# Loading the first K tile ahead of WQ and W1 in a DMA-bound attention decode kernel

## The chip, the cores and the metric

One core of a Trainium2 chip. The metric is the device time of one execution in microseconds (us). Within a comparison both kernels ran on the same chip; the experiments came in two batches on two chips, and the kernel before took 1272.90 us in one and 1272.82 us in the other. The changed kernel itself was not run again in these batches; where an experiment is set against it, the kernel before (1272.86 us beside it) is the link.

## The reference

The output mixes two branches with a gate: attention of one new token over a long K/V cache, and a small dense block.

```python
q = (x @ wq)                                     # x: 2 x 1 x 448, 16 query heads of 256
scores = einsum(q, repeat(k_cache, 2)) / 16      # k_cache: 2 x 8 x 32768 x 256, bf16
a = (softmax(scores) @ repeat(v_cache, 2)) @ wo  # v_cache: the same size
b = gelu(x @ w1 + b1) @ w2 + b2                  # 448 -> 1792 -> 448
g = sigmoid(sum(x * gate_w))
return g * a + (1 - g) * b
```

K and V are 268 MB each. Each byte of them is used once, so the kernel is a stream of loads with a little work behind it.

## The kernel before

In what follows PE is the matrix engine, DVE the vector engine, ACT the scalar engine, and SP the engine whose queue issues the big loads. Q is x @ WQ, and H is x @ W1, from which the GELU chain starts.

K and V are cut into 32 tiles each (128 partitions x 64 KB, 8.4 MB). A ring of three slots in on-chip memory takes them in turn. WQ and W1 first lie together in slot 0.

```python
        order = [("WQ", 0), ("W1", 0)]
        for i in range(NTILES + LAG):            # NTILES 32, LAG 2
            if i < NTILES:
                order.append(("K", i))
            if i >= LAG and i - LAG < LASTV:
                order.append(("V", i - LAG))
        # ... (tail: last V, W2, WO)
        rot = [d for d in order if d[0] in "KV" and d != ("V", LASTV)]
        for n, d in enumerate(rot):
            slot_of[d] = (n + 1) % NB            # NB 3: K0 slot 1, K1 slot 2, K2 slot 0, V0 slot 1, K3 slot 2, V1 slot 0
        # ...
        def released(d):                         # what frees the slot of tile d
            kind, idx = d
            return {"K": ("S", idx, NCK // 2 - 1), "V": ("PV", idx), "WQ": "QT", "W1": "HT"}[kind]
```

The load queue (SP) issues loads in that order and waits, before each, until the slot's last user is done:

```python
            for d in order:
                for pd in before_of[d]:          # the tiles that lay in the slot before
                    E.wait("pe", released(pd))
                # ... issue the load of d
```

So K2 waits for Q and H, which read WQ and W1 in slot 0; V0 for the scores of K0; K3 for the scores of K1; V1 for the scores of K2.

DVE has to transpose each K tile in place (eight instructions) before PE can compute its scores. Its program is in fixed order:

```python
            # prog_dve ... mask, gate (gp, gs, g, dg) ...
            E.wait_total("d_b")                            # the biases
            E.ins(... b2_f <- b2_bf)
            E.wait("pe", "GG")                             # gate matmuls; PE does them after Q
            E.ins(... g32); E.ins(... omB)
            gelu1()                                        # begins with E.wait("pe", "HT"): all of H
            gelu2()
            for i in range(LAG):
                K(i)                                       # wait for the K tile, 8 transposes; softmax at each group's end
            E.loop((NTILES - LAG) // UNIT, steps, ("dve", ("PT", 0)))
```

PE's program is in fixed order too: Q (waits for WQ), gate matmuls, H (waits for W1), then the scores of K0, and so on.

Of the kernel before, what the change touches and what calls it, by code (L numbers as in the profile page):

```python
# [125 lines left out]
def bass_gated_mix__gqa_block_cached__dense_activation_gelu__decode_kernel(  # L126
# [40 lines left out]
    NTILES = NG * NT  # L167
# [33 lines left out]
    with contextlib.ExitStack() as es:  # L201
# [70 lines left out]
        W_WQ, W_W1 = KC * HD + HW, KC * Fd + HF  # L272
        assert W_WQ + W_W1 <= SLOT and (NC + FC) * Dm <= SLOT
        LASTV = NTILES - 1
        order = [("WQ", 0), ("W1", 0)]
        for i in range(NTILES + LAG):
            if i < NTILES:
                order.append(("K", i))
            if i >= LAG and i - LAG < LASTV:
                order.append(("V", i - LAG))  # L280
# [561 lines left out]
```

## Time and profile before

The kernel took 1272.86 us in the median of six runs (1272.69 to 1272.92).

These lines are from the page of the kernel before: the span, the busy time of the engines, and, for 40 equal slices of the span, the busy tenths of the 16 DMA engines and the rate in GB/s.

```profile
span 1270.7 us, 8089 instructions
...
PE 701.6 (55%) x4544; PEld 146.4 (12%) x2016; DVE 685.8 (54%) x528; ACT 43.7 (3%) x183; POOL 3.3 (0%) x14
...
DMA  9999999999999999999999999999999999999998
GB/s 405 444 430 435 428 432 433 434 431 438 431 431 429 441 433 433 435 431 433 429 435 437 433 433 435 431 431 429 441 433 433 431 435 431 431 435 437 433 422 371
```

PE and DVE are about half idle; DMA is full in 39 of the 40 slices (the last is the kernel's end). The trace's DMA packets say it more sharply: a tile is 128 packets of 64 KB, each 2.42 us on one of the 16 engines, so 433 to 434 GB/s and 19.35 us a tile. Between 20 and 1200 us there is never a moment with fewer than 16 packets under way.

The chain of waits looks as if it named another limit (second line: share of the span by line):

```profile
DMA 63%; DVE 19%; PE 15%; issue 3%; SPq 0%; another core or an unknown queue 0%
DMA ring<-in_A_k_cache_dram 59%; DVE ring L722 17%; PE ps_s L490 5%; PE ps_s L335 4%; PE ps_o L335 4%; DMA ring<-in_A_wo_dram 3%; DVE mx L726 1%; PE ps_o L539 1%; PE ps_m L504 0%; PE ps_m L499 0%; DVE gmax L728 0%; DVE gmx L732 0%; SPq L383 0%; SPq L376 0%
```

It puts 17% on the transposes. To see whether they cost time, look at how early the loads are queued. The last number of these lines, from the DMA view, is the median time from issue to landing in us:

```profile
ring<-in_A_k_cache_dram SPq DMA_DIRECT2D x32, 49.7
ring<-in_A_v_cache_dram SPq DMA_DIRECT2D x31, 36.6
```

A tile needs 19.35 us of transfer. In the median a V load is therefore issued some 17 us, and a K load some 30 us, before the engines reach it. A transpose that ends later eats this slack first.

The part of the run that the change touches, on DVE (start in us, duration in us, instruction, in brackets the idle time before it and what ended that):

```profile
27.00 0.38 DVE L715 SCALAR_TENSOR_TENSOR hT_bf<-u_sb,omB,z_sb 128x14 bf16<-128x14 f32 x2
36.36 17.66 DVE L722 STREAM_TRANSPOSE ring<-ring 128x2048 uint32<-128x2048 uint32 x8 [8.99 <-DMA ring<-in_A_k_cache_dram]
55.72 17.66 DVE L722 STREAM_TRANSPOSE ring<-ring 128x2048 uint32<-128x2048 uint32 x8 [1.69 <-DMA ring<-in_A_k_cache_dram]
...
82.78 17.66 DVE L722 STREAM_TRANSPOSE ring<-ring 128x2048 uint32<-128x2048 uint32 x8 [0.23 <-DVE PT L739]
```

and on the load queue, in order WQ, W1, then K0 to K2, V0, K3, V1:

```profile
0.74 0.88 SPq L371 DMA_DIRECT2D ring<-in_A_wq_dram  x2
1.67 1.11 SPq L376 DMA_DIRECT2D ring<-in_B_w_dram  x2
2.81 22.79 SPq L393 DMA_DIRECT2D ring<-in_A_k_cache_dram  x3
57.76 0.33 SPq L393 DMA_DIRECT2D ring<-in_A_v_cache_dram  x1
77.11 0.33 SPq L393 DMA_DIRECT2D ring<-in_A_k_cache_dram  x1
104.17 0.33 SPq L393 DMA_DIRECT2D ring<-in_A_v_cache_dram  x1
```

The GELU chain is over at 27.4 us, DVE then idles 9 us for K0, and the transposes of K1 start as soon as K1 has landed (55.7). V1 is issued at 104.17 us. The engines finish their last packets of K3 between 111.4 and 113.7 us, so V1 is 7 us early.

### The profile page before, as it was taken

The page shows a single profiled execution, that of the slowest core. Times are in us where ns is not written, and L with a number is a line of the kernel's source. Part 1 is how long each engine was busy: PE and PEld are TensorE (multiplying, and loading weights), DVE is VectorE, ACT ScalarE, POOL GpSimd, SP SyncE. Part 2 cuts the span into 40 slices and gives each one's busy share as a digit, 9 for nine tenths or more (in the row PEclk, how much of TensorE's full clock was granted, in tenths as well). Part 3 has the DMA queues.
Part 4 walks back from the last instruction along what each step waited for, and adds up shares of the span by engine and source line. Part 5 has one row for each costly group of instructions (what it writes and reads, how often), then busy time and mean ns, then how long its engine had stood idle before and what let it go on. Part 6 is the DMA issues. An engine that isn't in the chain of part 4 may idle for free.

```text
span 1270.7 us, 8089 instructions
## 1 busy us (share of the span) xinstructions
PE 701.6 (55%) x4544; PEld 146.4 (12%) x2016; DVE 685.8 (54%) x528; ACT 43.7 (3%) x183; POOL 3.3 (0%) x14
## 2 busy tenths in 40 slices
PE   4666556644476454665545665445664436655465
PEld 3111111100011100111100111000110001111012
DVE  2875536655365563556735466453665636556341
ACT  1000000000000000000000000000000000000000
POOL 1000000000000000000000000000000000000000
PEclk9987788767787767887777787678877778876787
DMA  9999999999999999999999999999999999999998
GB/s 405 444 430 435 428 432 433 434 431 438 431 431 429 441 433 433 435 431 433 429 435 437 433 433 435 431 431 429 441 433 433 431 435 431 431 435 437 433 422 371
DMA packets 11116, 547.61 MB, mean 431 GB/s; under 512 B 1368, under 2 KB 1632, under 8 KB 2144
## 3 DMA queue, kind: packets, MB, share of 16 engines
q1 hardware_dynamic: 10948, 547.43, 99.7%
q8 instruction: 9, 0.15, 0.0%
q10 hardware_dynamic: 156, 0.01, 0.0%
q14 instruction: 3, 0.02, 0.0%
HBM read 547.43 MB, written 0.00 MB: 431 GB/s over the span
## 4 chain that ended last, share of the span: by engine, by line
DMA 63%; DVE 19%; PE 15%; issue 3%; SPq 0%; another core or an unknown queue 0%
DMA ring<-in_A_k_cache_dram 59%; DVE ring L722 17%; PE ps_s L490 5%; PE ps_s L335 4%; PE ps_o L335 4%; DMA ring<-in_A_wo_dram 3%; DVE mx L726 1%; PE ps_o L539 1%; PE ps_m L504 0%; PE ps_m L499 0%; DVE gmax L728 0%; DVE gmx L732 0%; SPq L383 0%; SPq L376 0%
## 5 line engine op out<-in xcount | busy, mean ns | idle before, releaser
L722 DVE STREAM_TRANSPOSE ring<-ring 128x2048 uint32<-128x2048 uint32 x256 | 565.2, 2275 | 385.1 <-DMA ring<-in_A_k_cache_dram 384.8
L490 PE MATMUL ps_s<-ring,Abd 128*128 128x512 bf16 x1024 | 426.5, 416 | 424.1 <-DVE ring L722 423.7
L335 PE MATMUL ps_s<-ring,Abd 128*128 128x512 bf16 x1024 | 422.5, 413 | 0.0
L490 PEld LDWEIGHTS ps_s<-ring,Abd 128*128 128x128 bf16 x1024 | 106.1, 104 | 846.8 <-DVE ring L722 475.4
L335 PE MATMUL ps_o<-ring,PT 128*24 128x512 bf16 x1504 | 115.4, 415 | 0.0
L539 PE MATMUL ps_o<-ring,PT 128*24 128x512 bf16 x544 | 58.9, 432 | 14.0 <-DMA ring<-in_A_v_cache_dram 14.0
L509 PE MATMUL ps_f<-o_sb,selg 128*32 128x257 f32 x32 | 17.0, 634 | 83.5 <-DVE o_sb L763 83.5
L763 DVE SCALAR_TENSOR_TENSOR o_sb<-ps_o,mask,o_sb 128x256 f32<-128x256 f32 x112 | 54.1, 483 | 9.9 <-PE ps_o L539 6.0
L726 DVE TENSOR_REDUCE mx<-ps_s 128x1 f32<-128x1024 f32 x16 | 19.6, 1224 | 59.8 <-PE ps_s L335 59.8
L636 ACT ACTIVATE negm<-ps_m 128x1 f32<-128x1 f32 x16 | 2.7, 171 | 1155.9 <-PE ps_m L504 1155.9
L739 DVE STREAM_TRANSPOSE PT<-pexp 128x1024 bf16<-128x1024 bf16 x16 | 19.9, 1244 | 41.1 <-PE ps_o L335 41.1
L539 PEld LDWEIGHTS ps_o<-ring,PT 128*24 128x24 bf16 x544 | 14.8, 100 | 108.0 <-issue 89.3
L736 DVE COPY ls<-lsum 128x1 f32<-128x1 f32 x16 | 2.5, 154 | 32.3 <-ACT pexp L640 32.3
L630 ACT COPY Abd<-qrep 32x16 bf16 (+1 forms) x128 | 19.5, 199 | 0.6
L640 ACT ACTIVATE pexp<-ps_s,negm 128x1024 bf16<-128x1024 f32 x16 | 17.8, 1114 | 1.7
L499 PE MATMUL ps_m<-ident_f,mx 128*1 128x128 f32 x32 | 6.1, 271 | 21.1 <-DVE mx L726 21.1
L760 DVE TENSOR_SCALAR o_sb<-ps_o,mask 128x256 f32<-128x256 f32 x16 | 7.6, 474 | 16.7 <-PE ps_o L335 16.7
L509 PEld LDWEIGHTS ps_f<-o_sb,selg 128*32 128x32 f32 x32 | 2.9, 140 | 101.9 <-DVE o_sb L763 99.8
L504 PE MATMUL ps_m<-ones_f,gmx 1*128 1x1 f32 x32 | 6.5, 272 | 9.9 <-DVE gmx L732 9.9
L728 DVE TENSOR_REDUCE gmax<-ps_m 1x2 f32<-1x128 f32 x16 | 4.5, 278 | 7.5 <-PE ps_m L499 7.5
L420 PE MATMUL ps_s<-xT,ring 128*128 128x2 bf16 x128 | 3.6, 165 | 8.0 <-DMA ring<-in_A_wq_dram 8.0
L504 PEld LDWEIGHTS ps_m<-ones_f,gmx 1*128 1x128 f32 x32 | 5.2, 201 | 14.6 <-DVE gmx L732 14.6
(76 smaller groups left out, 63.9 us busy)
## 6 DMA issues: line engine op xcount, KB each, us to landing
ring<-in_A_v_cache_dram SPq DMA_DIRECT2D x1, 4096.0 KB, 27.0
ring<-in_A_v_cache_dram SPq DMA_DIRECT2D x2, 2048.0 KB, 33.7
ring<-in_A_wq_dram SPq DMA_DIRECT2D x1, 3072.0 KB, 10.3
ring<-in_B_w_dram SPq DMA_DIRECT2D x1, 1568.0 KB, 34.3
ring<-in_A_wo_dram SPq DMA_DIRECT2D x1, 1568.0 KB, 37.7
ring<-in_B_w_dram SPq DMA_DIRECT2D x1, 1344.0 KB, 13.6
ring<-in_A_wo_dram SPq DMA_DIRECT2D x1, 1008.0 KB, 39.7
ring<-in_A_wo_dram SPq DMA_DIRECT2D x1, 560.0 KB, 40.5
```

What stands on the lines that cost most here:

```text
L335: return e.add_instruction(mybir.InstMatmult(name=f"I-{nc.next_id()}", engine=mybir.EngineType.PE, ldweights=False, ins=[e.lower_ap(x), e. ...
L490: fn = lambda e, o=o, x=x, st=st, sp=sp, s=s, w=w: e.matmul(o, a_win(s, w), x, start=st, stop=sp, skip_group_check=True)
L504: E.ins(lambda e: e.matmul(ps_m[:, C_BC:C_BC + 1], gmx[:, :], ones_f[0:1, 0:1], start=True, stop=True), key=("M2", g))
L509: E.ins(lambda e: e.matmul(ps_oa, selg[:, :], o_sb[:, :], start=False, stop=False, skip_group_check=True), key=("OT", g))
L539: fn = lambda e, o=o, x=x, wt=wt, st=st, sp=sp, j=j: e.matmul(o, wt, x, start=st, stop=sp, skip_group_check=True)
L630: E.ins(lambda e, o=o, Q=Q, c=c: e.copy(o[:, :, c:c + 2], qrep[32 * Q:32 * Q + 32, :, bass.ds(E.dyn(2 * g, 2), 2)]), key=(("A", g) if (Q = ...
L640: E.ins(lambda e: e.activation(pexp[:, :].rearrange("p (r i a) -> p i r a", r=CR, i=2), ps_s[:, :].rearrange("p (i r a) -> p i r a", i=2, ...
L722: E.ins(lambda e: e.transpose(k_words(idx, blk), k_words(idx, blk)), key=("T", idx, blk))
L726: E.ins(lambda e: e.tensor_reduce(mx[:, :], ps_s[:, :], AX.X, ALU.max), key=("MX", g))
L739: E.ins(lambda e: e.transpose(PT[:, :], pexp[:, :]), key=("PT", g))
L760: E.ins(lambda e, p=p, m=m: e.tensor_scalar(o_sb[:, 0:Dh], p, m, None, op0=ALU.mult), key=("OS0", g))
L763: E.ins(lambda e, p=p, m=m: e.scalar_tensor_tensor(out=o_sb[:, 0:Dh], in0=p, scalar=m, in1=o_sb[:, 0:Dh], op0=ALU.mult, op1=ALU.add), key= ...
```

## The change

The first K tile is loaded first, so that the big stream begins at once and the first transposes could begin earlier, while WQ and W1 arrive behind it.

```diff
-        order = [("WQ", 0), ("W1", 0)]
+        order = [("K", 0), ("WQ", 0), ("W1", 0)]
         for i in range(NTILES + LAG):
-            if i < NTILES:
+            if 0 < i < NTILES:
                 order.append(("K", i))
```

No slot, byte or instruction is added or removed, and the order on PE, DVE and ACT stays.

## The prediction

> **What bounds the kernel now.** The DMA engines. The page shows 547.6 MB in a span of 1270.7 us, 431 GB/s, and DMA 9 tenths busy or more in 39 of 40 slices. In the trace's DMA packets every K or V tile is 128 packets of 64 KB, 2.42 us each on 16 engines (434 GB/s), 19.35 us a tile; from 20 to 1200 us there are never fewer than 16 under way. The Trainium skill ("DMA: Bandwidth & Descriptors", Specifications) gives a fabric ceiling of 435 GB/s; this trace agrees. PE (55%) and DVE (54%) are far from full. The chain of waits names K loads, transposes and score matmuls, but issue to landing is 36.6 us (V) and 49.7 us (K) in the median: loads are queued early, so those waits are slack.
>
> **What the change moves.** Only the SP queue: the first K load goes from fifth to first. Bytes, instructions and ring slots stay; PE, DVE and ACT keep their order. K0 should land 14 us earlier (36.4 to about 22 us), WQ and W1 about 19 us later (WQ 12.4 to about 31, W1 16 to about 35). K1, K2, V0, K3 land as before (K1 55.7, K2 75, V0 94.7, K3 114.1).
>
> The early K0 buys nothing, because DVE's program puts the gate, the bias and the GELU chain ahead of the first transpose, and these need Q and H from PE. By the timeline's durations: WQ at 31 + 3.6 (Q) + 2.0 (copy, spread, gates) gives about 37; H takes 6.8, to 44; the GELU chain 2.2. The first transpose starts at about 46 instead of 36.4: **10 us later, not 14 earlier**. T(K0) and T(K1) take 17.7 each, now back to back (46 to 81.5); scores of K1 end at about 85 (before 77.1), the softmax takes 5.7, T(K2) starts at about 91 (before 82.8), and the scores of K2 end at about 112.5 (before 104.2).
>
> **How much of it is on the critical path.** Does the DMA run dry?
> - K2's load waits for H: about 44, while K1 streams until 55. Slack 9.
> - V0 waits for the scores of K0: about 67.5 (before 57.8); needed at 72.7. Slack 5.
> - K3: about 85; needed at 92. Slack 7.
> - V1 waits for the scores of K2: about 112.5. The engines run out of K3 between 111.4 and 113.7 us, and issue to first packet took 1.0 us at the start. Early engines may idle 1 to 2 us, the last ones 0. This is the only exposed place: 0 to 1.5 us, once, never given back.
> Then T(K3) waits for its data at 114 as before, and all is in step again. The tail is unchanged.
>
> The small loads on ACT's queue now alternate with 64 KB packets (round robin per packet: same page, "Queues, rings and completion order"), so the biases land at about 25 us instead of 12; they are needed at 36.
>
> **Predicted:** 1273.2 us, range 1272.3 to 1275.0. Faster by over 2%: 0.5%; within 2%: 98.5%; slower by over 2%: 1%.
>
> **What would show it:** first K landing near 22 us, first transpose near 46, released by H; V1's issue at 111 to 114; at most a short dip of DMA near 113; later landings shifted by that dip alone; the last slices the same.
>
> **What would make it wrong:** an H chain longer by several us (V1 later, DMA idle by as much), a small load starved behind K0, or another start-up cost of the first packets for 64 KB than for 24 KB rows.

## The result, and the profile after

| | kernel before | changed kernel |
|---|---|---|
| median of 6 runs, us | 1272.86 | 1274.85 |
| range, us | 1272.69 to 1272.92 | 1274.53 to 1275.31 |

The ratio is 1.0016, with a 95% interval of 1.0003 to 1.0029: 2.0 us slower, which counts as the same at 2%. A ratio is the mean time of one kernel's runs over that of the other's runs of the same rounds, so it is not quite the ratio of the medians.

The same lines of the page, for the changed kernel:

```profile
span 1272.8 us, 8089 instructions
...
DMA  9999999999999999999999999999999999999998
GB/s 399 452 433 400 427 431 430 443 437 427 430 437 428 437 441 430 430 430 435 430 445 430 433 428 437 428 441 437 430 430 430 435 430 443 433 433 428 437 423 370
```

One slice stands out: the fourth, 95 to 127 us, fell from 435 to 400 GB/s, and nothing like it follows. 35 of 435 GB/s in a slice of 31.8 us are about 2.6 us of transfers, a rough figure, since slices with nothing wrong differ by several GB/s. DVE in the changed kernel:

```profile
30.20 0.38 DVE L691 CAST gp_sb<-PT 2x448 f32<-2x448 bf16 x1 [12.66 <-DMA PT<-in_B_b_dram]
37.16 0.15 DVE L693 COPY g<-ps_m 32x1 f32<-32x1 f32 x1 [6.57 <-PE ps_m L469]
...
44.33 0.25 DVE L699 TENSOR_TENSOR z_sb<-ps_m,b1T 128x14 f32<-128x14 f32 x2 [6.96 <-PE ps_m L443]
...
46.41 35.20 DVE L722 STREAM_TRANSPOSE ring<-ring 128x2048 uint32<-128x2048 uint32 x16
...
91.01 17.66 DVE L722 STREAM_TRANSPOSE ring<-ring 128x2048 uint32<-128x2048 uint32 x8 [0.23 <-DVE PT L739]
```

K0's last packet ended at 22.5 us, but the first transpose starts at 46.4. In between DVE waits in turn for the biases, for the gate matmuls behind Q (WQ is there at 31.6), and for H. Then K0 and K1 are transposed back to back (16 instructions, 35.2 us), as K1 has been waiting since 55.4. The load queue:

```profile
0.74 0.41 SPq L393 DMA_DIRECT2D ring<-in_A_k_cache_dram  x1
1.20 0.92 SPq L371 DMA_DIRECT2D ring<-in_A_wq_dram  x2
2.16 1.08 SPq L376 DMA_DIRECT2D ring<-in_B_w_dram  x2
3.28 41.43 SPq L393 DMA_DIRECT2D ring<-in_A_k_cache_dram  x2
67.79 0.33 SPq L393 DMA_DIRECT2D ring<-in_A_v_cache_dram  x1
85.33 0.33 SPq L393 DMA_DIRECT2D ring<-in_A_k_cache_dram  x1
112.40 0.33 SPq L393 DMA_DIRECT2D ring<-in_A_v_cache_dram  x1
```

V1 is issued at 112.40 us, 8.2 us later than before. Its first packet starts at 113.39, and 12 of the 16 engines were done with K3 between 111.6 and 112.1. Worked out from the trace's DMA packets, the engines idle 1.51 us in the mean there, and at no other moment between 20 and 1200 us. Besides, the 16 first packets of V1 took 2.4 to 3.4 us instead of 2.42, which is 0.59 us per engine over the tile. Together 2.1 us; the span grew by 2.1. (This sum is a mean over the 16 engines, while the end of the run follows the last of them. That the two agree so well is partly chance, as the section on the prediction shows.)

### The profile page after: what moved, and what is told of

Same layout as the page of the kernel before. It is cut to its first block, busy times and chain, and to the rows that moved or that the text cites. A ratio compares the mean times of both kernels' runs of the same rounds, so it can differ in the third digit from the quotient of the medians.

```text
span 1272.8 us, 8089 instructions
## 1 busy us (share of the span) xinstructions
PE 698.9 (55%) x4544; PEld 146.4 (12%) x2016; DVE 685.6 (54%) x528; ACT 43.7 (3%) x183; POOL 3.3 (0%) x14
## 4 chain that ended last, share of the span: by engine, by line
DMA 59%; DVE 22%; PE 15%; issue 3%; another core or an unknown queue 2%; SPq 0%; ACT 0%; DVEq 0%
DMA ring<-in_A_k_cache_dram 53%; DVE ring L722 19%; PE ps_s L490 4%; PE ps_s L335 4%; PE ps_o L335 4%; DMA ring<-in_A_wo_dram 3%; DMA ring<-in_A_wq_dram 2%; DVE mx L726 1%; PE ps_o L539 1%; PE ps_m L504 0%; PE ps_m L499 0%; DVE gmax L728 0%; PE ps_m L439 0%; PE ps_s L420 0%
```

## The experiments

Two theories and a third reading were put against each other. **Theory D**: the loss is DMA idle time ahead of V1, made by DVE's fixed order, which holds the first transposes back until H is done. **Rival R**: loading K0 first costs by itself, at the start (first packets, small loads behind 64 KB packets), wherever DVE stands. **Rival C**: the chain of waits taken at its word, the transposes are on the critical path.

All eight kernels gave correct results and were timed in five rounds beside the kernel before.

### a_gelu_late: the GELU chain behind the first tile's transposes

```diff
 # the changed kernel, DVE's program
-            gelu1()
-            gelu2()
             for i in range(LAG):
                 K(i)
+                if i == 0:
+                    gelu1()
+                    gelu2()
```

> The changed kernel, but DVE does the GELU chain after the transposes of the first K tile instead of ahead of them. Theory D (the 2 us are DMA idle time at V1, because the first transposes wait 10 us longer for H): the first transpose starts at about 37.5 us, once the gate copies are done, instead of 46.4; the transposes of the second K tile at about 57.3; V1 is issued at about 106 instead of 112.4; no DMA engine idles there and the time is 1272.9 us, within 0.4. Rival R (loading K0 ahead of the weights costs 2 us by itself at the start, through the first packets or the small loads behind them, wherever DVE stands): the time stays at 1274.8.

Measured: 1273.01 us, before 1272.90 (ratio 1.0002, 0.9988 to 1.0015). DVE and the load queue of this kernel (the first fence DVE, the second V1's issue):

```profile
37.08 17.64 DVE L722 STREAM_TRANSPOSE ring<-ring 128x2048 uint32<-128x2048 uint32 x8
...
56.67 4.50 DVE L722 STREAM_TRANSPOSE ring<-ring 128x2048 uint32<-128x2048 uint32 x2
```

```profile
105.13 0.33 SPq L393 DMA_DIRECT2D ring<-in_A_v_cache_dram  x1
```

The load order is the changed one, the loss is gone, and no DMA engine idles between 20 and 1200 us. R falls. The changed kernel's own packets agree: its 16 engines end K1 at 53.96 us in the mean, those of the kernel before at 53.94, so loading K0 first had cost nothing by then. The only thing undone is that DVE waits for H ahead of its transposes.

### a_k0_early: the transposes of K0 as soon as it lands

```diff
 # the changed kernel, DVE's program (T moved up; the loop over K(0) then skips them)
+            for blk in range(NCK):
+                T(0, blk)
             E.wait_total("d_b")
             E.ins(... b2_f <- b2_bf)
```

> The changed kernel, but DVE does the transposes of the first K tile as soon as it has landed, ahead of the bias cast, the gate copies and the GELU chain, which is what an early K0 is good for. Theory D: the first transpose starts at about 23 us, 13 us earlier than in the kernel before, H runs about 3 us later than in the changed kernel, V1 is issued near 104 us, no DMA engine idles, and the time is 1272.9 us, within 0.4: no faster than before, as the DMA engines were already full. Rival R: 1274.8. A reader who believes that the first transposes are on the critical path (rival C, the chain of waits taken at its word) expects a gain of up to 10 us: 1263 to 1270.

Measured: 1272.85 us, before 1272.90 (ratio 1.0001, 0.9987 to 1.0015). The first transposes on DVE:

```profile
22.56 17.66 DVE L662 STREAM_TRANSPOSE ring<-ring 128x2048 uint32<-128x2048 uint32 x8 [5.00 <-DMA ring<-in_A_k_cache_dram]
...
55.73 4.50 DVE L662 STREAM_TRANSPOSE ring<-ring 128x2048 uint32<-128x2048 uint32 x2 [5.99 <-DMA ring<-in_A_k_cache_dram]
```

They start 13.8 us earlier than in the kernel before, and the time does not move. K1 lands at 55.3 us all the same, and DVE idles 6 us for it. So the change's intent, even carried through, is worth nothing here, and C falls for these first tiles (the transposes of later tiles were not moved by a run of their own).

### b_delay3 and b_delay6: a delay on DVE without the change

A delay was put ahead of the first transpose in the kernel before: fills of a tile in PSUM (the memory in which PE leaves its sums) that is zero already, each waiting for the one before. (By the author's account a first form without these waits had a write-after-write race and was mended before it went to the chip.)

```diff
 # the kernel before, DVE's program
             gelu1()
             gelu2()
+            for n in range(3):                  # 6 in b_delay6, 8 in b_delay8, 9 in b_delay9
+                E.wait("dve", ("dl", n - 1) if n else "o0")
+                E.ins(lambda e: e.memset(ps_o[:, :], 0.0), key=("dl", n))
```

> The kernel before with its own load order, and three idle fills of a PSUM tile on DVE (about 1.76 us each, 5.3 in all) ahead of the first transpose. Theory D: the first transpose starts at about 41.7 us, the transposes of the second K tile at about 59.4 (3.6 late), V1 is issued at about 107.9, before the engines run out of K3 at 111.4: no cost, 1272.9 us within 0.4. Rival C (transposes on the critical path): 1278. Rival R: 1272.9.

> The same with six fills (10.6 us), the delay that the change gave to the first transpose, without the change. Theory D: the first transpose starts at about 47 us, V1 is issued at about 113, its first packets start at about 114, the engines idle 2.1 us in the mean, the first packets after the pause cost another 0.6, and the time is 1275.4 us (1274.5 to 1276.3): the change's loss without the change's load order. Rival R: 1272.9. Rival C: 1283.

Measured: 1272.98 us and 1272.87 us, before 1272.90 (ratios 1.0000 and 1.0000). Both doses missed what was expected of them: DVE was idle from 27.4 to 36.4 us, as the lines of the kernel before show, so three fills vanished in that idle time, and six moved the first transpose to 40.8 and V1's issue to 106.74 us only. The time of b_delay3 met its expectation by luck alone, since its first transpose moved by 0.1 us, and it tests nothing. b_delay6 still speaks against C: 4.4 us of delay on the first transpose cost nothing.

### b_delay8 and b_delay9: the dose corrected

> The runs with three and six fills were dosed wrongly: DVE was idle from 27.4 to 36.4 us in the kernel before, so three fills fell into idle time and six delayed the first transpose by 4.4 us only (40.8). A fill costs 2.27 us with its wait. Eight fills: first transpose at 45.3 us; V1 is issued 66.0 us after the first transpose (so in the changed kernel, 46.4 and 112.4, and with six fills, 40.8 and 106.7), so at 111.3, first packets at 112.3. Theory D: the 13 engines that are done with K3 by 111.9 idle about 0.6 us, the last ones nothing; the time is 1273.3 us (1272.8 to 1273.8). Rival R (the load order itself): 1272.9.

> The kernel before with nine fills: first transpose at 47.6 us, V1 issued at 113.6, first packets at 114.6. Theory D: mean idle of the 16 engines about 2.5 us, 0.6 more for the first packets after the pause; the slowest engine, done with K3 at 113.7, loses 1 us of pause and 0.6 of restart: 1275.5 us (1274.8 to 1276.2), the change's loss without the change's order. Rival R: 1272.9. If it stays at 1272.9 theory D falls.

Measured: eight fills 1274.19 us (1273.86 to 1275.20), nine fills 1276.57 us (1276.19 to 1276.79), before 1272.82 (1272.58 to 1273.07). The ratios are 1.0012 (0.9998 to 1.0025) and 1.0028 (1.0015 to 1.0042). Two lines of the run with nine fills, from DVE and from the load queue:

```profile
47.73 35.17 DVE L722 STREAM_TRANSPOSE ring<-ring 128x2048 uint32<-128x2048 uint32 x16
```

```profile
114.27 0.33 SPq L393 DMA_DIRECT2D ring<-in_A_v_cache_dram  x1
```

And the rate by slices on its page, where again only the fourth slice falls:

```profile
GB/s 405 436 438 369 428 451 434 426 432 431 438 440 428 428 438 428 440 438 428 430 436 428 444 434 428 430 436 428 446 432 428 436 430 434 442 430 428 438 423 369
```

The loss appears in the kernel before, with its own load order, once V1 comes too late. That is D. Both runs cost more than expected, by 0.9 and 1.1 us, and their medians lie above the stated ranges; the text below the table says where that comes from.

### a_delay3: more delay on the changed kernel

The same three fills in the changed kernel, where DVE has no idle time there.

> The changed kernel with three fills ahead of the first transpose, where DVE has no idle time left: first transpose at 53.2 us, V0 issued near 74.6 and V1 near 119.2. Theory D: past the slack every us of delay is a us of DMA idle time: 1281.7 us (1280.5 to 1282.5), 6.8 more than the change. Rival R: 1274.9, as the transposes have nothing to do with it.

Measured: 1281.44 us, before 1272.82 (ratio 1.0072, 1.0058 to 1.0085). Past the slack a us on DVE is about a us of the kernel: the first transpose came 6.5 us later than in the changed kernel (52.88 against 46.41) and the time is 6.6 us higher (1274.85 there, measured in another batch). V0 is late as well now: 2.2 of 7.2 us of mean idle time lie ahead of V0, the rest ahead of V1.

### k0_between: half the change

```diff
-        order = [("WQ", 0), ("W1", 0)]
+        order = [("WQ", 0), ("K", 0), ("W1", 0)]
         for i in range(NTILES + LAG):
-            if i < NTILES:
+            if 0 < i < NTILES:
```

> Half the change: WQ first, then K0, then W1. Q is then early but H still waits for W1, which lands at about 35 us: H from 35.7 to 42.5, first transpose at about 44.7, V1 issued at about 110.7, first packets at 111.7. Theory D: the engines idle 0.1 us or less, the time is 1273.0 us (1272.7 to 1273.4), though K0 still lands 10 us earlier than before and the first transpose 8.3 us later. Rival R: in between, about 1273.8.

Measured: 1274.69 us (1273.85 to 1275.58), before 1272.82 (ratio 1.0014, 1.0000 to 1.0027). Not the 1273.0 expected: V1's issue came at 111.37 us instead of 110.7, as the first transpose started at 45.17. This run alone would not tell D from R; beside b_delay8, whose V1 is issued at the same moment with the old load order, it does. V1's issue in k0_between (first line) and in b_delay8 (second line), then the table of all kernels:

```profile
111.37 0.33 SPq L393 DMA_DIRECT2D ring<-in_A_v_cache_dram  x1
111.30 0.33 SPq L393 DMA_DIRECT2D ring<-in_A_v_cache_dram  x1
```

| kernel | V1 issued, us | mean DMA idle, 20 to 1200 us | slow packets of V0 and V1, us per engine | last packet of V30, against before | span, against before |
|---|---|---|---|---|---|
| before | 104.17 | 0 | 0 | (1236.00) | (1270.7) |
| b_delay3 | 104.25 | 0 | 0 | 0.0 | 0.0 |
| a_k0_early | 104.73 | 0 | 0 | 0.0 | 0.0 |
| a_gelu_late | 105.13 | 0 | 0 | 0.0 | +0.2 |
| b_delay6 | 106.74 | 0 | 0 | +0.2 | +0.2 |
| b_delay8 | 111.30 | 0.48 | 0.74 | +2.2 | +2.2 |
| k0_between | 111.37 | 0.71 | 0.58 | +2.5 | +2.5 |
| changed | 112.40 | 1.51 | 0.59 | +2.1 | +2.1 |
| b_delay9 | 114.27 | 3.20 | 0.66 | +3.8 | +3.9 |
| a_delay3 | 118.84 | 7.18 | 1.31 | +8.4 | +8.4 |

All columns are of each kernel's profiled run. The third sums the missing packets below 16 over time, divided by 16. The fourth is what the packets of V0 and V1 took beyond 2.421 us, summed and divided by 16 (0.08 us or less counts as 0). The fifth is when the slowest engine ended its last full V tile, near the end of the run. The order of the rows is that of V1's issue, not that of the load orders. The medians of the runs follow it: from b_delay8 to a_delay3 they lie 1.4, 1.9, 2.0, 3.8 and 8.6 us above the kernel before. By their 95% intervals alone b_delay8 and k0_between are not clear of no loss, but each of their five runs is slower than each of the nine of the kernel before (1273.85 and more against 1273.07 and less), and their traces show the idle engines.

In the three deep doses idle time and slow packets, as means over the engines, add up to the growth of the span. The span itself follows the last engine, and that it lost as much as the mean is partly chance: in the profiled runs of b_delay9 and a_delay3 the last engine ended V1 1.1 us after the next one, and by the packets' times it was held up by a block on the queue that the profile calls "instruction" (see the last point of the next section). That is the size by which b_delay9 missed its expectation, but no run tests it. In the two shallow ones (0.5 and 0.7 us of mean idle) the last engine lost about 1 us more than the mean: in b_delay8 one engine started its first packet of V1 at 114.26 and needed 4.0 us for it, and in k0_between one started it at 115.39, when the others had begun by 113.5. Why these single engines were so late stays open. The five runs of these two kernels lie 1.3 and 1.7 us apart, those of b_delay9 0.6 and those of a_delay3 1.9.

## Why the prediction was right or wrong

The time lay in the range (1272.3 to 1275.0), 0.15 us from its upper end; the central value, 1273.2, was 1.7 us too low. That the number is in the range is partly luck: the loss that the prediction worked out, 0 to 1.5 us, was exceeded (2.0 us), and only the wider margin of the range held it.

- **The DMA engines bound the kernel: right.** The time grows only where the DMA engines lose time, and neither 13.8 us earlier transposes (a_k0_early) nor 4.4 us later ones (b_delay6) move it. The Trainium skill's fabric ceiling of 435 GB/s ("DMA: Bandwidth & Descriptors", Specifications) is what a tile's packets reach: 433 to 434 GB/s.
- **K0 14 us earlier, first transpose 10 us later: right.** K0's last packet ended at 22.5 us (said: about 22), the first transpose started at 46.41 (said: about 46), released by H. a_gelu_late shows that without this wait the loss is gone (1273.01 us).
- **V1's issue is the only exposed place: right.** Said about 112.5 us, measured 112.40; its first packet 1.0 us later, as said. K2, V0 and K3 lost nothing.
- **The small loads: right in kind.** The bias pieces of 28 bytes ended at 25.8 us (said: about 25; before 11.0), alternating with the big packets of the load queue (64 KB of K0, then 24 KB of WQ), as the skill's round robin per packet says (same page, "Queues, rings and completion order"). The last bias row came later than said: its packets started at 27.6 and 29.5 us, and DVE cast it at 30.20. It was needed at 36, so this cost nothing.
- **"Early engines may idle 1 to 2 us, the last ones 0 ... 0 to 1.5 us": this term was too small.** Two things were left out of the sum. First, the restart: after the pause the first packets took up to 3.4 us instead of 2.42, 0.59 us per engine, as at the start of the kernel, where K0's packets cost 0.69 us more than steady ones. That cost was in the trace before (its first sixteen 24 KB packets took 1.1 to 2.3 us, steady ones 0.9). The prediction named it as a risk at the start and did not carry it to the pause. Second, the central value, 0.3 us above the kernel before, took the last engine as untouched and as the only one that counts. Before, the engines ended a tile spread over 2.3 us, and the last lay 1.5 us behind the mean (113.67 against 112.15). The pause pulled them together: at the end of V1 the last was only 0.6 us behind the mean, but the mean was 2.1 us late, and the last 1.2.
- **What made the last engine's 1.2 us into 2.0.** At 133.60 us a 16 KB packet of the queue that the profile calls "instruction" took 0.90 us. By the packets' times (the trace does not name the engine) it fell on an engine that had ended V1 at that very moment, started K4 0.89 us late at 134.49 with a packet that took 2.96 us instead of 2.42, and was then the last to end K4: 154.37, 2.0 us later than the last of the kernel before, and 0.8 later than the next engine (153.60). In the kernel before, the like packet at 130.99, with a 2.96 us packet behind it too, fell on an engine that was far ahead of the last, and did not show. In b_delay9 and a_delay3 such blocks, at 133.03 and 135.05 us, lead in the same way to the engine that ended V1 last (136.87 and 141.31). In all ten traces a 64 KB packet of 2.96 us or slightly more starts where the block of that time ends. This reading rests on matching times and was not tested by a run of its own.

No kernel of these beats the kernel before. Between 20 and 1200 us it leaves no idle DMA engine that a load order could win back; whether one could gain in the first 20 us or in the last 70 was not tested.

## What to carry to other kernels

When the DMA engines are full, as here, ask of each load not "when does the data come" but "how early is it queued", and compute for a reordering which issue loses its lead; here the loss was nothing up to the slack (V1 issued 2.6 us later cost nothing) and about one for one beyond it (6.4 us later than in the changed kernel cost 6.6 more). A load moved ahead helps only if its consumer's program can take it: look at what stands in front of the consumer in its engine's fixed order (here a chain that waits for weights which the move made later). When a pause of the DMA is close, count the restart as well, not the pause alone.

## What the Trainium skill lacked or had wrong

- No page gives a cost for restarting a DMA stream that ran dry. Here it was 0.58 to 0.74 us per engine on 64 KB packets, for mean pauses between 0.5 and 5 us: the first packets took 2.4 to 3.5 us instead of 2.42 (one of them 4.0). It belongs to "DMA: Bandwidth & Descriptors". Why the first packets are slow stays open.
- The same page gives a first-byte latency of about 0.6 us for loads issued from SP (Specifications) without saying from when it counts. Here the first packet starts 0.95 to 1.03 us after the start of the issuing instruction; the issue itself takes 0.33 to 0.41 us, so from its end it is about 0.6 us, which agrees.
- "Runtime: NRT & Kernel Launch" (Instruction fetch mechanics) says that instructions are fetched in blocks of 16 KiB on a DMA queue of their own and calls the cost mostly hidden. The blocks are there (16,384 bytes, 0.9 to 1.3 us each, 8 or 9 in a run), but by the times of the packets they take their time from the engines that move the data: one block and the slower packet behind it took 1.4 us from its engine, and made the changed kernel's last engine 0.8 us later.
